# Folding the Nyquist bin of a DFT convolution into the empty sine column, and issuing one weight load later

## The chip, the cores and the metric

The kernel runs on one core of a Trainium2 chip. The metric is device time in microseconds (us) of one execution. The 13 executions of the kernel before lie within 0.3% of their median of 502.65 us (501.42 to 503.08). Every ratio below is the mean time of one kernel's fast runs over the mean of the other kernel's fast runs of the same rounds, so it is not quite the ratio of the medians that are quoted. In a profile, PE is TensorE's matmul unit, PEld its weight load, DVE is VectorE, ACT is ScalarE, and a name with q (SPq, ACTq) is that engine's queue issuing a DMA. The granted clock is the share of TensorE's full clock that the chip allowed (1.00 is full, 0.50 half). L567 is line 567 of the kernel; the changed kernel has other line numbers, so groups are best recognised by their tiles.

## The reference, cut to what matters

```python
def _A_ref(q, k, v, shift_k, ssm_k, ssm_D):       # B=1, S=2048, D=640, bf16 inputs
    k_shift = sum(k_pad[:, t:t+S, :] * shift_k[:, ks-1-t] for t in range(ks))   # 4 taps
    kv = k_shift * v
    y = irfft(rfft(pad(kv)) * rfft(pad(ssm_k)))[:S]          # causal convolution of length 2S
    return q * (y + kv * ssm_D)

x = A_q
h = x + _A_ref(layernorm(x), A_k, A_v, A_shift_k, A_ssm_k, A_ssm_D)
return h + (silu(n @ w_gate) * (n @ w_up)) @ w_down          # n = layernorm(h), F = 1728
```

## The kernel before

The convolution is done with matmuls. Even and odd time positions are two sequences of H = 1024; each is transformed with a 1024 x 1024 cosine table and a sine table, in eight blocks of 128 frequencies. The cosine half and the sine half of a block are called its two planes. The order of the work is: transposes of `ssm_k`; six "K blocks" (transform of the filter); "X blocks" (transform of kv), with the last two K blocks between them; a spectral product for each block on VectorE; the inverse transform in 16 groups, each followed by an output step on VectorE; then gate/up and down matmuls, twice.

The sine table has only 1024 frequencies, 0 to 1023. The 1025th, the Nyquist frequency, alternates +1, -1, and is done apart:

```python
def nyq_groups(src_fn, dep_all, scale, dstrow):
    for par in range(2):
        for c, (ch0, cw) in enumerate(chunks):          # chunks of 384 and 256 columns
            for tt in range(NT):                        # 8 tiles; altvec is one column of +1, -1
                tok = pe.op(... t.matmul(o, altvec, r, start=st, stop=sp_) ...)      # 32 matmuls
            atok = act.op(... a.activation(out=dst, in_=src, func=ACTF.Copy, scale=scale) ...)
...
nyqK_toks = nyq_groups(kt_chunk, t_kt_all, 0.5 / H, nyqK)     # before the first K block
...
for Fb in range(NF - NKDEF): emit_kfwd(Fb)                    # six K blocks
nyqX_toks = nyq_groups(kv_chunk, t_kv_all, 1.0, nyqX)         # before the first X block
# four one-row products on VectorE make AHrow from nyqX and nyqK
...
for Fb in range(NF):
    X_done[Fb] = fwd_block(Fb, kv_chunk, ...)                 # X block
    if Fb < NKDEF: emit_kfwd(NF - NKDEF + Fb)                 # K blocks 6 and 7
    ab_done[Fb] = spectral_products(Fb, ...)                  # VectorE
```

In the inverse, each group ends with two matmuls of one row (`altrow`, AHrow) that add the Nyquist part. The weights are loaded when the spectral products are done, all on ScalarE's queue and on one semaphore. The output step of each group uses ScalarE for a tiny square root:

```python
dma(Wg_sb, ..., s_w, deps=wdeps, eng=act)
dma(Wu_sb, ..., s_w, deps=wdeps, eng=act)
dma(Wd_sb[:, 0:NFB - 1, :], ..., s_w, deps=wdeps, eng=act)
t_wall = dma(Wd_sb[0:FL, NFB - 1, :], ..., s_w, deps=wdeps, eng=act)
...
def y_output(...):                                            # one per inverse group
    ...                                                       # L753: PSUM + kv*D, two pieces
    t_ag = dve.op(... bn_aggr ...)                            # statistics of h
    t_sq = act.op(... a.activation(out=sq2, in_=ls2[:, 1:2], func=ACTF.Sqrt, ...), deps=[t_ag, ...])
    t_rs = dve.op(... v.reciprocal ...)                       # L764, waits for the square root
    t_hn = dve.op(...)                                        # the normalised h
```

## Time and profile before

The median was 502.4 us in the first 4 runs and 502.65 us over 13.

| stage | us from the span's start | what sets the pace |
|---|---|---|
| loads, transposes, shift matmuls | 0 to 35.0 | DMA |
| K Nyquist rows | 35.0 to 41.5 | TensorE |
| six K blocks | 41.5 to 93.8 | TensorE |
| X Nyquist rows | 93.8 to 98.8 | TensorE |
| X blocks 0 to 2, K blocks 6 and 7 | 98.8 to 145 | TensorE |
| products 2 to 7 | 145.2 to 212.5 | VectorE |
| inverse and outputs | 212.6 to 309 | VectorE, 5.37 us a step |
| gate/up, down, twice | 309 to 501 | TensorE |

The page of the kernel before, part 4: the chain that ended last, followed back from the last instruction, by engine and by line, as shares of the span.

```profile
PE 61%; DVE 27%; SPq 4%; issue 2%; ACT 2%; DMA 2%; DVEq 0%
PE ps L567 19%; PE ps L877 13%; PE ps L836 12%; DVE r_x L628 11%; PE ps L834 11%; SPq L313 4%; PE ps L723 3%; DVE r_x L753 3%; DMA r_x<-in_A_k_dram 2%; PE ps L533 2%; DVE r_stage L628 2%; DVE r_x L756 2%; DVE kvt L757 2%; DVE st L759 1%; DVE r_k L765 1%
```

The removed groups (L533) are on that chain. The timeline of the kernel before around them: start, duration, engine, line, operation, tiles and shapes, count, and in brackets the idle time before the first of them and who ended it.

```profile
33.27 1.78 PE L461 MATMUL ps<-r_x,shiftm 128*128 128x384 bf16 x6 [7.57 <-DMA r_x<-in_A_k_dram]
...
34.98 5.96 PE L533 MATMUL ps<-r_k,alt 128*1 128x384 bf16 x32
...
41.49 20.70 PE L567 MATMUL ps<-r_k,tabs 128*128 128x384 bf16 x151 [0.55 <-ACT rows L536]
...
93.75 4.51 PE L533 MATMUL ps<-kvt,alt 128*1 128x384 bf16 x32
...
98.81 8.85 PE L567 MATMUL ps<-kvt,tabs 128*128 128x384 bf16 x64 [0.55 <-ACT rows L536]
```

The same 32 matmuls took 5.96 us the first time and 4.51 us the second. The reason is TensorE's clock. The view of stretches, kernel before: stretch, its length, busy time (and number of instructions) of PE, PEld, DVE, ACT and POOL, then the granted PE clock, the DMA share and GB/s.

```profile
33.00:35.00 2.00, 1.73 (x7) 0.76 (x8) 2.00 (x6) 1.20 (x4) 0.00 (x0) 0.50 1.05 395
35.00:37.00 2.00, 2.00 (x8) 0.82 (x8) 2.00 (x6) 0.89 (x3) 0.00 (x0) 0.50 1.05 386
...
39.00:41.00 2.00, 1.94 (x15) 1.02 (x13) 2.00 (x6) 0.68 (x3) 0.00 (x0) 1.00 1.05 393
```

The clock was 0.50 until some way into the stretch after 37 us.

The timeline of the kernel before, first operation of products 0, 1 and 2:

```profile
110.44 0.83 DVE L628 TENSOR_TENSOR r_x<-r_x 128x1280 bf16<-128x1280 bf16 x1 [9.19 <-ACT r_x L580]
...
127.82 0.83 DVE L628 TENSOR_TENSOR r_x<-r_x 128x1280 bf16<-128x1280 bf16 x1 [6.28 <-ACT r_x L580]
...
145.21 0.83 DVE L628 TENSOR_TENSOR r_x<-r_x 128x1280 bf16<-128x1280 bf16 x1 [6.28 <-ACT r_x L580]
```

After that the products follow one another, 11.24 us each. And the timeline of the kernel before at the start of the inverse: the issue of the W_down load, the PSUM addition (L753) of the first, second and third output, and the first square root with the reciprocal behind it.

```profile
213.61 13.22 ACTq L313 DMA_DIRECT2D r_x<-in_B_w_down_dram  x2
...
218.91 0.89 DVE L753 TENSOR_TENSOR r_x<-ps,r_x 128x384 bf16<-128x384 f32 x2 [2.88 <-PE ps L730]
...
226.87 0.29 ACT L763 ACTIVATE sqv<-lnstat,epsv 128x1 f32<-128x1 f32 x1 [30.67 <-issue]
227.20 0.16 DVE L764 RECIPROCAL lnstat<-sqv 128x1 f32<-128x1 f32 x1 [5.12 <-ACT sqv L763]
...
228.91 0.89 DVE L753 TENSOR_TENSOR r_x<-ps,r_x 128x384 bf16<-128x384 f32 x2
...
234.28 0.89 DVE L753 TENSOR_TENSOR r_x<-ps,r_x 128x384 bf16<-128x384 f32 x2
```

The W_down issue holds ScalarE's queue for 13.22 us. It is two transfers: the first, 2080 KB, was issued in 0.55 us, and the second, 80 KB and the fourth on this queue, held it from 214.19 to 226.82 (the two starts and lengths stand in the packed trace; the view merges them). The square root stands behind it in program order and runs at 226.87, although its statistics were done at 222.1. VectorE waits 5.12 us for it. From then on a step takes 5.37 us (228.91 to 234.28).

### The profile page before, as it was taken

The page shows a single profiled execution, that of the slowest core. Times are in us where ns is not written, and L with a number is a line of the kernel's source. Part 1 is how long each engine was busy: PE and PEld are TensorE (multiplying, and loading weights), DVE is VectorE, ACT ScalarE, POOL GpSimd, SP SyncE. Part 2 cuts the span into 40 slices and gives each one's busy share as a digit, 9 for nine tenths or more (in the row PEclk, how much of TensorE's full clock was granted, in tenths as well). Part 3 has the DMA queues.
Part 4 walks back from the last instruction along what each step waited for, and adds up shares of the span by engine and source line. Part 5 has one row for each costly group of instructions (what it writes and reads, how often), then busy time and mean ns, then how long its engine had stood idle before and what let it go on. Part 6 is the DMA issues. An engine that isn't in the chain of part 4 may idle for free.

```text
span 501.0 us, 6952 instructions
## 1 busy us (share of the span) xinstructions
PE 437.2 (87%) x2794; PEld 266.6 (53%) x2806; DVE 325.8 (65%) x622; ACT 134.4 (27%) x298; POOL 0.3 (0%) x5
## 2 busy tenths in 40 slices
PE   0739999999999892099999996999989999998997
PEld 0516777677777561066666662444446644443564
DVE  1499998127749999937888888666632256666122
ACT  0632444554477444000000002222200022222000
POOL 0000000000000000000000000000000000000000
PEclk9969999999999897589999999999999999999899
DMA  6999410000000000096001100000001100000011
GB/s 239 393 391 335 147 54 2 0 1 1 0 1 2 0 1 0 1 371 226 27 27 40 27 27 1 1 0 1 0 15 41 39 14 0 2 0 0 26 42 39
DMA packets 16992, 31.78 MB, mean 63 GB/s; under 512 B 1664, under 2 KB 8768, under 8 KB 16960
## 3 DMA queue, kind: packets, MB, share of 16 engines
q1 hardware_dynamic: 13888, 24.70, 14.0%
q10 hardware_dynamic: 3072, 6.64, 3.5%
q8 instruction: 22, 0.36, 0.3%
q14 instruction: 10, 0.08, 0.1%
HBM read 28.71 MB, written 2.62 MB: 63 GB/s over the span
## 4 chain that ended last, share of the span: by engine, by line
PE 61%; DVE 27%; SPq 4%; issue 2%; ACT 2%; DMA 2%; DVEq 0%
PE ps L567 19%; PE ps L877 13%; PE ps L836 12%; DVE r_x L628 11%; PE ps L834 11%; SPq L313 4%; PE ps L723 3%; DVE r_x L753 3%; DMA r_x<-in_A_k_dram 2%; PE ps L533 2%; DVE r_stage L628 2%; DVE r_x L756 2%; DVE kvt L757 2%; DVE st L759 1%; DVE r_k L765 1%
## 5 line engine op out<-in xcount | busy, mean ns | idle before, releaser
L836 PE MATMUL ps<-r_k,r_kpl 128*128 128x512 bf16 (+1 forms) x280 | 107.2, 383 | 1.0 <-DVE r_x L753 0.3
L834 PE MATMUL ps<-r_k,r_kpl 128*128 128x512 bf16 (+1 forms) x268 | 102.7, 383 | 4.2 <-DVE tabs L847 2.9
L723 PE MATMUL ps<-r_stage,tabs 128*128 128x384 bf16 (+1 forms) x512 | 73.5, 303 | 23.9 <-DVE r_stage L628 21.6
L567 PE MATMUL ps<-kvt,tabs 128*128 128x384 bf16 (+1 forms) x512 | 72.0, 304 | 3.6 <-ACT r_x L580 3.1
L723 PEld LDWEIGHTS ps<-r_stage,tabs 128*128 128x128 bf16 x512 | 49.4, 99 | 45.8 <-DVE r_stage L628 21.9
L567 PE MATMUL ps<-r_k,tabs 128*128 128x384 bf16 (+1 forms) x512 | 70.0, 300 | 0.6 <-ACT rows L536 0.6
L877 PE MATMUL ps<-r_x,tabs 128*128 128x384 bf16 x448 | 66.0, 305 | 4.0 <-DVE tabs L847 4.0
L844 DVE TENSOR_TENSOR r_kpl<-ps,r_kpl 128x512 bf16<-128x512 f32 (+1 forms) x56 | 38.7, 691 | 42.5 <-ACT r_kpl L842 42.5
L842 ACT ACTIVATE r_kpl<-ps 128x512 bf16<-128x512 f32 (+1 forms) x56 | 33.2, 597 | 120.3 <-PE ps L834 118.5
L567 PEld LDWEIGHTS ps<-kvt,tabs 128*128 128x128 bf16 x512 | 50.5, 99 | 24.8 <-ACT r_x L580 3.7
L567 PEld LDWEIGHTS ps<-r_k,tabs 128*128 128x128 bf16 x512 | 50.0, 98 | 20.2 <-issue 0.8
L877 PEld LDWEIGHTS ps<-r_x,tabs 128*128 128x128 bf16 x448 | 41.9, 99 | 28.4 <-issue 8.9
L885 DVE TENSOR_TENSOR r_x<-ps,kvt 128x384 bf16<-128x384 f32 (+1 forms) x32 | 14.2, 486 | 53.9 <-PE ps L877 53.9
L834 PEld LDWEIGHTS ps<-r_k,r_kpl 128*128 128x128 bf16 (+1 forms) x280 | 27.8, 99 | 39.0 <-DVE tabs L847 4.2
L628 DVE TENSOR_TENSOR r_x<-r_x,r_kpl 128x2560 bf16<-128x2560 bf16 x32 | 46.2, 1486 | 0.3
L628 DVE TENSOR_TENSOR r_x<-r_x 128x1280 bf16<-128x1280 bf16 x40 | 31.5, 819 | 22.4 <-ACT r_x L580 21.7
L836 PEld LDWEIGHTS ps<-r_k,r_kpl 128*128 128x128 bf16 (+1 forms) x280 | 27.8, 99 | 32.5 <-issue 1.1
L847 DVE TENSOR_TENSOR tabs<-ps,r_kpl 128x512 bf16<-128x512 f32 (+1 forms) x56 | 38.7, 691 | 1.9
L577 ACT ACTIVATE r_kpl<-ps,sck 128x384 bf16<-128x384 f32 x64 | 28.5, 528 | 40.2 <-PE ps L567 40.2
L577 ACT ACTIVATE r_x<-ps 128x384 bf16<-128x384 f32 x64 | 25.4, 458 | 33.7 <-PE ps L567 31.2
L763 ACT ACTIVATE sqv<-lnstat,epsv 128x1 f32<-128x1 f32 x16 | 4.7, 295 | 106.7 <-DVE lnstat L761 76.0
L580 ACT ACTIVATE r_x<-ps,tw 128x384 bf16<-128x384 f32 (+1 forms) x64 | 31.5, 572 | 0.0
(56 smaller groups left out, 248.5 us busy)
## 6 DMA issues: line engine op xcount, KB each, us to landing
r_stage<-in_A_k_dram SPq DMA_DIRECT2D x15, 320.0 KB, 7.4
r_k<-in_A_ssm_k_dram SPq DMA_DIRECT2D x5, 512.0 KB, 8.3
r_stage<-in_A_q_dram SPq DMA_DIRECT2D x8, 320.0 KB, 6.0
r_stage<-in_A_v_dram SPq DMA_DIRECT2D x8, 320.0 KB, 6.5
r_x<-in_A_q_dram SPq DMA_DIRECT2D x16, 160.0 KB, 2.3
out_dram<-r_x SPq DMA_DIRECT2D x16, 160.0 KB, 1.8
r_kpl<-in_B_w_gate_dram ACTq DMA_DIRECT2D x1, 2160.0 KB, 9.9
r_kpl<-in_B_w_up_dram ACTq DMA_DIRECT2D x1, 2160.0 KB, 15.2
```

What stands on the lines that cost most here:

```text
L313: return e.op_inc(lambda g, d=dst, s=src: g.dma_start(d, s), sem, 16, deps=deps)
L567: t.matmul(o, l, r, start=st, stop=sp_),
L577: atok = act.op(lambda a, o=dst, s=src, sc=sc: a.activation(out=o, in_=s, func=ACTF.Copy, scale=sc), deps=[last[gi]] + list(extra_act_deps))
L580: atok = act.op(lambda a, o=sdst[:, ch0:ch0 + cw], s=src, sc=ssc: a.activation(out=o, in_=s, func=ACTF.Copy, scale=sc), deps=list(sdeps))
L628: tt = lambda o, a, b2, op, dd: dve.op(lambda v: v.tensor_tensor(out=o, in0=a, in1=b2, op=op), deps=dd)
L723: last = pe.op(lambda t, o=o, l=lhsT, r=r, st=first: t.matmul(o, l, r, start=st, stop=False), deps=deps if (first and c == 0) else ())
L834: lastG = pe.op(lambda t, o=oG, l=lg, r=rhs, st=st, sp_=sp_: t.matmul(o, l, r, start=st, stop=sp_), deps=deps if dti == 0 else ())
L836: lastU = pe.op(lambda t, o=oU, l=lu, r=rhs, st=st, sp_=sp_: t.matmul(o, l, r, start=st, stop=sp_))
L842: t_sg = act.op(lambda a, o=sgb, s=oG: a.activation(out=o, in_=s, func=ACTF.Sigmoid), deps=[lastG, gu_pair_done.get(pidx - 3)])
L844: t_gs = dve.op(lambda v, o=gsb, s=oG, g=sgb: v.tensor_tensor(out=o, in0=s, in1=g, op=ALU.mult), deps=[t_sg, gu_pair_done.get(pidx - 3)])
L847: t_gu = dve.op(lambda v, o=dstgu, s=oU, g=gsb: v.tensor_tensor(out=o, in0=s, in1=g, op=ALU.mult), deps=[t_gs, lastU] + guT_war_deps)
L877: last = pe.op(lambda t, o=o, l=lhsT, r=r, st=first, sp_=(ft == NFB - 1): t.matmul(o, l, r, start=st, stop=sp_), deps=deps if (first and c ...
```

## The change

The sine of frequency 0 is zero at all times, so its column of the sine table carries nothing. The change puts the alternating signs there: a copy of the first 128 columns of the sine table, with that column replaced (`s0f`, 256 KB), serves block 0's sine plane, and a copy of the first 128 rows (`si0`, 256 KB) serves the inverse. The Nyquist bin then rides along in the row of frequency 0. Row 0 of the product mixes two real bins as if they were one complex bin, so it is computed again with one-row operations. The change also gives the transposes eight PSUM banks instead of four, and moves the W_down load behind the seventh inverse group, onto a semaphore of its own.

```diff
+        s0f_np = stab_f[:, 0:P].copy();  s0f_np[:, 0] = altn       # forward: block 0's sine plane
+        si0_np = stab_f[0:P, :].copy();  si0_np[0, :] = altn       # inverse: block 0's sine rows
+        def load_s0f_stab():
+            bulk_tok["s0f"] = dma(s0f[:], ..., s_s0f)               # ahead of the 2 MB sine table
+            return dma(stab, ..., s_tab2)
-                bank = tg % 4
+                bank = tg % 8
-        nyqK_toks = nyq_groups(kt_chunk, t_kt_all, 0.5 / H, nyqK)
-        nyqX_toks = nyq_groups(kv_chunk, t_kv_all, 1.0, nyqX)
-        q1 ... q4                                                    # one-row Nyquist products
+                    lhsT = s0f[:, tt, :] if (Fb == 0 and pl == 1) else tab[:, tt, Fb * P:(Fb + 1) * P]
+                  lambda Fb_, pl: (sck[:, 0:1] if Fb_ == 0 else sck[:, 1:2])   # row 0's scale 0.5/H now in both planes of K block 0
+            if Fb == 0:                                              # 8 one-row copies on ScalarE
+                scaled.setdefault((par, pl), []).append((xrow0[0:1, poff:poff + D], 1.0, []))
 ...
+            if Fb == 0:                                              # 6 one-row repairs on VectorE
+                f1 = ... xrow0 * krow0 ;  f2, f3 = ... ;  f4 = ... ;  f5, f6 = ...
 ...
-        if NFB > 1:
-            dma(Wd_sb[:, 0:NFB - 1, :], ..., s_w, deps=wdeps, eng=act)
-        t_wall = dma(Wd_sb[0:FL, NFB - 1, :], ..., s_w, deps=wdeps, eng=act)
 ...
-            for c, (ch0, cw) in enumerate(chunks):                   # inverse: two one-row matmuls a group
-                toks.append(pe.op(... t.matmul(o, altrow, r, start=False, stop=True)))
 ...
+                if qi == 6:
+                    dma(Wd_sb[:, 0:NFB - 1, :], ..., s_wd, deps=wdeps, eng=act)
+                    t_wall = dma(Wd_sb[0:FL, NFB - 1, :], ..., s_wd, deps=wdeps, eng=act)
```

More of the change, by code (lines that the diff above doesn't have):

```diff
@@ L149, in bass_sequential_preLN__ssm_conv_h3__swiglu_ffn__prompt_kernel @@
     ctab_np = _to_bf16(np.cos(ang))
-    stab_np = _to_bf16(np.sin(ang))
+    stab_f = np.sin(ang)
+    stab_np = _to_bf16(stab_f)
+    altn = (-1.0) ** np.arange(H)
+    s0f_np = stab_f[:, 0:P].copy()
+    s0f_np[:, 0] = altn
+    si0_np = stab_f[0:P, :].copy()
+    si0_np[0, :] = altn
+    s0f_np = _to_bf16(s0f_np)
+    si0_np = _to_bf16(si0_np)
     maxshift = 2
@@ L163, in bass_sequential_preLN__ssm_conv_h3__swiglu_ffn__prompt_kernel @@
     sck_np[0, 0] = 0.5 / H
-    alt_np = np.ones((P, 2 * P), dtype=np.float32)
-    alt_np[:, 0] = (-1.0) ** np.arange(P)
-    alt_np[0, P:2 * P] = (-1.0) ** np.arange(P)
-    alt_np = _to_bf16(alt_np)
     ctab_dram = nc.inline_tensor(ctab_np, name="cst_ctab")
@@ L173, in bass_sequential_preLN__ssm_conv_h3__swiglu_ffn__prompt_kernel @@
     sck_dram = nc.inline_tensor(sck_np, name="cst_sck")
-    alt_dram = nc.inline_tensor(alt_np, name="cst_alt")
+    s0f_dram = nc.inline_tensor(s0f_np, name="cst_s0f")
+    si0_dram = nc.inline_tensor(si0_np, name="cst_si0")
     bf, f32 = dt.bfloat16, dt.float32
@@ L189, in bass_sequential_preLN__ssm_conv_h3__swiglu_ffn__prompt_kernel @@
         ident = shiftm[:, 0:P]
-        alt = sb("alt", [P, 2 * P], bf)
-        altvec = alt[:, 0:1]
-        altrow = alt[0:1, P:2 * P]
         tw = sb("tw", [P, NF, 4], f32)
+        s0f = sb("s0f", [P, NT, P], bf)
+        si0 = sb("si0", [P, H], bf)
         sck = sb("sck", [P, 2], f32)
@@ L201, in bass_sequential_preLN__ssm_conv_h3__swiglu_ffn__prompt_kernel @@
         sqv2 = sb("sqv2", [P, 2, NT], f32)
-        rows = sb("rows", [P, 6 * D], bf)
-        nyqK = rows[0:1, 0:2 * D]
-        nyqX = rows[0:1, 2 * D:4 * D]
-        AHrow = rows[0:1, 4 * D:6 * D]
         NSTG = 3
@@ L220, in bass_sequential_preLN__ssm_conv_h3__swiglu_ffn__prompt_kernel @@
         a1tmp = [r_stage[:, a1tmp_off + i * D:a1tmp_off + (i + 1) * D] for i in range(4)]
-        nyqT = r_stage[0:1, a1tmp_off:a1tmp_off + 4 * D]
         AB = r_stage[:, 0:NF * 4 * D].rearrange("p (f x) -> p f x", f=NF)
@@ L231, in bass_sequential_preLN__ssm_conv_h3__swiglu_ffn__prompt_kernel @@
         NXR, NHN = 2, 3
-        sz_k = NCB * S + NHN * D
+        sz_k = NCB * S + max(NHN, 4) * D
         r_k = sb("r_k", [P, sz_k], bf)
+        xrow0 = r_k[0:1, NCB * S:NCB * S + 4 * D]
         kc = r_k[:, 0:NCB * S].rearrange("p (c s) -> p c s", c=NCB)
@@ L307, in bass_sequential_preLN__ssm_conv_h3__swiglu_ffn__prompt_kernel @@
         s_w = mksem("s_w")
+        s_wd = mksem("s_wd")
         s_xr = [mksem(f"s_xr{i}") for i in range(NXR)]
@@ L336, in kc_load @@
             kc_tok[cb] = dma(kc[:, cb, :], A_ssm_k[cb * P:(cb + 1) * P, :], s_kcb[cb])
+        s_s0f = mksem("s_s0f")
+        s_si0 = mksem("s_si0")
+        def load_s0f_stab():
+            bulk_tok["s0f"] = dma(s0f[:], s0f_dram.ap().rearrange("(t p) f -> p t f", p=P), s_s0f)
+            return dma(stab, stab_dram.ap().rearrange("(t p) f -> p t f", p=P), s_tab2)
         bulk = [
             ("ctab", lambda: dma(ctab, ctab_dram.ap().rearrange("(t p) f -> p t f", p=P), s_tab)),
-            ("stab", lambda: dma(stab, stab_dram.ap().rearrange("(t p) f -> p t f", p=P), s_tab2)),
+            ("stab", load_s0f_stab),
+            ("si0", lambda: dma(si0[:], si0_dram.ap(), s_si0)),
         ]
@@ L343, in bass_sequential_preLN__ssm_conv_h3__swiglu_ffn__prompt_kernel @@
         dma(shiftm[:], shift_dram.ap(), s_const)
-        dma(alt[:], alt_dram.ap(), s_const)
         dma(tw[:], tw_dram.ap(), s_const)
@@ L348, in bass_sequential_preLN__ssm_conv_h3__swiglu_ffn__prompt_kernel @@
         t_const = dma(Wtab[:], A_shift_k.partition_broadcast(P), s_const)
-        t_ident = t_alt = t_tw = t_sck = t_D = t_W = t_const
+        t_ident = t_tw = t_sck = t_D = t_W = t_const
         pairs = list(range(1, NT)) + [0]
@@ L520, in bass_sequential_preLN__ssm_conv_h3__swiglu_ffn__prompt_kernel @@
         t_stab = bulk_tok["stab"]
+        t_s0f = bulk_tok["s0f"]
         t_kv_all = dve.sem.cur()
-        def nyq_groups(src_fn, dep_all, scale, dstrow):
-            atoks = []
-            for par in range(2):
-                for c, (ch0, cw) in enumerate(chunks):
-                    bank = par * NCH + c
-                    deps = [dep_all, t_alt, bank_rd.get(bank)]
-                    tok = None
-                    for tt in range(NT):
-                        o = bank32(bank, 0, cw)[0:1]
-                        tok = pe.op(lambda t, o=o, r=src_fn(par, tt, c), st=(tt == 0), sp_=(tt == NT - 1):
-                                    t.matmul(o, altvec, r, start=st, stop=sp_), deps=deps if tt == 0 else ())
-                    dst = dstrow[0:1, par * D + ch0:par * D + ch0 + cw]
-                    src = bank32(bank, 0, cw)[0:1]
-                    atok = act.op(lambda a, o=dst, s=src: a.activation(out=o, in_=s, func=ACTF.Copy, scale=scale), deps=[tok])
-                    bank_rd[bank] = atok
-                    atoks.append(atok)
-            return atoks
         def kt_chunk(par, tt, c):
@@ L554, in fwd_block @@
                 base = (g2 % 2) * 4
-                deps = [dep_all, (t_ctab if pl == 0 else t_stab)]
+                deps = [dep_all, t_s0f if (Fb == 0 and pl == 1) else (t_ctab if pl == 0 else t_stab)]
                 for k4 in range(2 * NCH):
@@ L559, in fwd_block @@
                 for tt in range(NT):
-                    lhsT = tab[:, tt, Fb * P:(Fb + 1) * P]
+                    lhsT = s0f[:, tt, :] if (Fb == 0 and pl == 1) else tab[:, tt, Fb * P:(Fb + 1) * P]
                     for par in range(2):
@@ L579, in fwd_block @@
                         for (sdst, ssc, sdeps) in extra_copies:
-                            atok = act.op(lambda a, o=sdst[:, ch0:ch0 + cw], s=src, sc=ssc: a.activation(out=o, in_=s, func=ACTF.Copy, scale=sc),
+                            npart = sdst.shape[0]
+                            atok = act.op(lambda a, o=sdst[:, ch0:ch0 + cw], s=src[0:npart], sc=ssc: a.activation(out=o, in_=s, func=ACTF.Copy, scale=sc),
                                           deps=list(sdeps))
@@ L591, in emit_kfwd @@
             K_done[Fb] = fwd_block(Fb, kt_chunk, t_kt_all,
-                                   Kpl[:, Fb, :], lambda Fb_, pl: (sck[:, 0:1] if (Fb_ == 0 and pl == 0) else sck[:, 1:2]),
+                                   Kpl[:, Fb, :], lambda Fb_, pl: (sck[:, 0:1] if Fb_ == 0 else sck[:, 1:2]),
                                    extra_act_deps=[t_sck])
@@ L598, in bass_sequential_preLN__ssm_conv_h3__swiglu_ffn__prompt_kernel @@
         emit_ln1_rstd()
-        nyqX_toks = nyq_groups(kv_chunk, t_kv_all, 1.0, nyqX)
-        ndeps = nyqK_toks + nyqX_toks
-        ndeps = ndeps + [t_kv_all]
-        nxv = nyqX.rearrange("p (a x) -> p a x", a=2)
-        q1 = dve.op(lambda v: v.tensor_tensor(out=nyqT[0:1, 0:2 * D].rearrange("p (a x) -> p a x", a=2), in0=nxv,
-                                             in1=nyqK.rearrange("p (a x) -> p a x", a=2), op=ALU.mult), deps=ndeps)
-        q2 = dve.op(lambda v: v.tensor_tensor(out=nyqT[0:1, 2 * D:4 * D].rearrange("p (a x) -> p a x", a=2), in0=nxv,
-                                             in1=_rev_segments(nyqK, 2), op=ALU.mult), deps=ndeps)
-        q3 = dve.op(lambda v: v.tensor_tensor(out=AHrow[0:1, 0:D], in0=nyqT[0:1, 0:D], in1=nyqT[0:1, D:2 * D], op=ALU.subtract), deps=[q1])
-        q4 = dve.op(lambda v: v.tensor_tensor(out=AHrow[0:1, D:2 * D], in0=nyqT[0:1, 2 * D:3 * D], in1=nyqT[0:1, 3 * D:4 * D], op=ALU.add), deps=[q2])
-        t_nyq_done = q4 if q4.val > q3.val else q3
         ab_done = {}
@@ L673, in bass_sequential_preLN__ssm_conv_h3__swiglu_ffn__prompt_kernel @@
             }
+            if Fb == 0:
+                for (par, pl) in ((0, 0), (0, 1), (1, 0), (1, 1)):
+                    poff = (2 * par + pl) * D
+                    scaled.setdefault((par, pl), []).append((xrow0[0:1, poff:poff + D], 1.0, []))
             X_done[Fb] = fwd_block(Fb, kv_chunk, t_kv_all,
@@ L677, in bass_sequential_preLN__ssm_conv_h3__swiglu_ffn__prompt_kernel @@
                 emit_kfwd(NF - NKDEF + Fb)
-            ab_done[Fb] = spectral_products(Fb, Xpl[slot], Kpl[:, Fb, :], deps=[X_done[Fb], K_done[Fb], t_tw, t_nyq_done], ostok=X_done[Fb])
+            ab_done[Fb] = spectral_products(Fb, Xpl[slot], Kpl[:, Fb, :], deps=[X_done[Fb], K_done[Fb], t_tw], ostok=X_done[Fb])
+            if Fb == 0:
+                krow0 = Kpl[0:1, 0, :]
+                ab0 = AB[0:1, 0, :]
+                fx_deps = [ab_done[0], X_done[0], K_done[0]]
+                fixTb = SV1[0:1, 0:4 * D]
+                f1 = dve.op(lambda v: v.tensor_tensor(out=fixTb, in0=xrow0[0:1, 0:4 * D], in1=krow0[0:1, 0:4 * D], op=ALU.mult), deps=fx_deps)
+                f2 = dve.op(lambda v: v.tensor_tensor(out=ab0[0:1, 0:D], in0=fixTb[0:1, 0:D], in1=fixTb[0:1, 2 * D:3 * D], op=ALU.add), deps=[f1])
+                f3 = dve.op(lambda v: v.tensor_tensor(out=ab0[0:1, 2 * D:3 * D], in0=fixTb[0:1, D:2 * D], in1=fixTb[0:1, 3 * D:4 * D], op=ALU.subtract), deps=[f1])
+                f4 = dve.op(lambda v: v.tensor_tensor(out=fixTb, in0=xrow0[0:1, 0:4 * D], in1=_rev_segments(krow0[0:1, 0:4 * D], 2), op=ALU.mult), deps=[f2, f3])
+                f5 = dve.op(lambda v: v.tensor_tensor(out=ab0[0:1, D:2 * D], in0=fixTb[0:1, 0:D], in1=fixTb[0:1, 2 * D:3 * D], op=ALU.add), deps=[f4])
+                f6 = dve.op(lambda v: v.tensor_tensor(out=ab0[0:1, 3 * D:4 * D], in0=fixTb[0:1, D:2 * D], in1=fixTb[0:1, 3 * D:4 * D], op=ALU.add), deps=[f4])
+                ab_prev_reads[0] = ab_prev_reads[0] + [f5, f6]
+                t_fix = f6
         t_ab_all = ab_done[NF - 1]
@@ L682, in bass_sequential_preLN__ssm_conv_h3__swiglu_ffn__prompt_kernel @@
         dma(Wg_sb, B_w_gate.rearrange("(t p) f -> p t f", p=P), s_w, deps=wdeps, eng=act)
-        dma(Wu_sb, B_w_up.rearrange("(t p) f -> p t f", p=P), s_w, deps=wdeps, eng=act)
-        if NFB > 1:
-            dma(Wd_sb[:, 0:NFB - 1, :], B_w_down[0:(NFB - 1) * P, :].rearrange("(t p) d -> p t d", p=P), s_w, deps=wdeps, eng=act)
-        t_wall = dma(Wd_sb[0:FL, NFB - 1, :], B_w_down[(NFB - 1) * P:(NFB - 1) * P + FL, :], s_w, deps=wdeps, eng=act)
-        t_wg = t_wu = t_wd = t_wd2 = t_wall
-        inv_deps_all = [t_ab_all, t_nyq_done]
+        t_wgu = dma(Wu_sb, B_w_up.rearrange("(t p) f -> p t f", p=P), s_w, deps=wdeps, eng=act)
+        t_wg = t_wu = t_wgu
+        inv_deps_all = [t_ab_all, bulk_tok["si0"]]
         xr_free = [None] * NXR
@@ L712, in inverse_group @@
                 deps.append(bank_rd.get(bnk))
-            last = None
             first = True
             ab_c = par * D
+            nmm = NF * 2 * NCH
+            cnt = 0
+            lasts = [None] * NCH
             for Ft in range(NF):
@@ L718, in inverse_group @@
                     tab = ctab if pl == 0 else stab
-                    lhsT = tab[:, Ft, tb * P:(tb + 1) * P]
+                    lhsT = si0[:, tb * P:(tb + 1) * P] if (Ft == 0 and pl == 1) else tab[:, Ft, tb * P:(tb + 1) * P]
                     for c, (ch0, cw) in enumerate(chunks):
@@ L722, in inverse_group @@
                         r = AB[:, Ft, pl * 2 * D + ab_c + ch0:pl * 2 * D + ab_c + ch0 + cw]
-                        last = pe.op(lambda t, o=o, l=lhsT, r=r, st=first: t.matmul(o, l, r, start=st, stop=False),
-                                     deps=deps if (first and c == 0) else ())
+                        cnt += 1
+                        lasts[c] = pe.op(lambda t, o=o, l=lhsT, r=r, st=first, sp_=(cnt > nmm - NCH): t.matmul(o, l, r, start=st, stop=sp_),
+                                         deps=deps if (first and c == 0) else ())
                     first = False
-            toks = []
-            for c, (ch0, cw) in enumerate(chunks):
-                o = bank32(banks[c], 0, cw)
-                r = AHrow[0:1, par * D + ch0:par * D + ch0 + cw]
-                toks.append(pe.op(lambda t, o=o, r=r: t.matmul(o, altrow, r, start=False, stop=True)))
-            return banks, toks[-1]
+            return banks, lasts[-1]
         def y_output(qi, par, tb, banks, ytok):
@@ L806, in bass_sequential_preLN__ssm_conv_h3__swiglu_ffn__prompt_kernel @@
                     x_reload(qi + NXR)
+                if qi == 6:
+                    if NFB > 1:
+                        dma(Wd_sb[:, 0:NFB - 1, :], B_w_down[0:(NFB - 1) * P, :].rearrange("(t p) d -> p t d", p=P), s_wd, deps=wdeps, eng=act)
+                    t_wall = dma(Wd_sb[0:FL, NFB - 1, :], B_w_down[(NFB - 1) * P:(NFB - 1) * P + FL, :], s_wd, deps=wdeps, eng=act)
+                    t_wd = t_wd2 = t_wall
                 gi += 1
```

## The prediction

> **What bounds the kernel now.** The chain of waits shows four stages in series. (1) TensorE from 33.3 us, when the last small input lands: shift matmuls, K Nyquist rows (32 one-column matmuls, 35.0 to 41.0), six K blocks (41.5 to 93.8), X Nyquist rows (93.8 to 98.3), then X and deferred K blocks to 142.7. (2) VectorE: six spectral products back to back, 145.2 to 212.5. (3) Inverse transform to 304: VectorE's output steps, one per 5.37 us (timeline); TensorE needs 4.5 us for a group's 32 matmuls, 0.44 for the Nyquist pair, 0.45 for transposes, just less. (4) Gate/up and down matmuls, TensorE-bound, to 501.
>
> **What the change does.**
> - Removes the K Nyquist matmuls (5.9 us plus a 0.55 us wait for ScalarE) and the X ones (4.45 plus 0.55). All lie on the chain, but not all is won. The windows show the granted clock at 0.5 from 33 to 37.5 us, and the removed matmuls sat in 2.5 us of that. [...] So the K blocks inherit the slow stretch: about 1.4 us given back. Win 5.0 + 5.0 = 10.0 us. VectorE's kv phase ends at 85.2, before X starts at about 88.8.
> - Removes 32 Nyquist matmuls from the inverse groups (10 us busy). Hidden behind VectorE's 5.37 us step, except in the first group: 0.4 us.
> - Moves the W_down load behind the seventh group, off the weights' semaphore. Its issue holds ScalarE's queue from 213.6 to 226.8 (timeline), so the first tiny square root runs at 226.9 and VectorE waits 5.1 us for it, once (waits). VectorE sets the pace afterwards, so this is never recovered. Without it the second output's addition moves from 228.9 to about 223.5; TensorE, now slightly behind, takes back about 0.5. Win 4.9 us.
> - Adds, in X block 0, eight one-row copies on ScalarE (0.37 us each by the present row copies: 1.5 per plane). ScalarE then needs 4.6 us per plane against TensorE's 4.35: a stall of about 0.4.
> - Adds six one-row VectorE operations after product 0. A row costs what 128 do (1x1280 took 0.815 us, 128x1280 0.819), so 4.8 us, but VectorE idles 6.3 us before product 1 and again before product 2. Cost: zero.
> - Adds two 256 KB loads. The first is needed by K block 0's second plane at about 40.7; the loads ahead of it land at 37.0, so I estimate 38.5. The larger table lands a microsecond after 43.2, needed at 49.
> - Eight transpose banks instead of four: the shift matmuls still wait for a load until 33.2. Zero.
>
> **Sum.** 502.4 - 10.0 - 0.4 - 4.9 + 0.4 - 0.2 (one small load fewer) = **487.3 us**; 8 in 10: 484.5 to 490.8. Chances: faster by over 2% 0.93, within 2% 0.06, slower 0.01.
>
> **What would show it.** First K matmul near 35 us, at clock 0.5 for 2 to 3 us; first X matmul near 88.8; still 6 x 11.24 us of products before the inverse, which starts near 203; first square root within 1 us of its statistics; output steps still 5.37 us, VectorE-paced; gate/up and down unchanged. Wrong would be: K block 0 waiting for the small sine table, steps below 5.3 us, or products 1 or 2 waiting on the row repairs.
>
> **What would make it wrong.** The small table's 256-byte rows landing after 41 us, the W_down issue blocking ScalarE again, or the slow clock returning elsewhere.

A mark shows where a sentence was cut; no term of the sum is cut with it, and it comes to 487.3 us as it stands. That the K blocks inherit the slow stretch, and the 1.4 us given back for it, was the author's estimate from the 2.5 us of clock 0.50 in which, by the view of stretches, the removed matmuls sat (35.0 to 37.5; the clock record has the half clock until 37.97). The prediction gives no source for the 0.2 us of the small load.

## More of the kernel before

The trace's clock record has half clock from 27.73 us, while TensorE idled (25.70 to 33.27), until 37.97. From the first shift matmul at 33.27 until then TensorE was busy without a break, for 4.70 us. What brings the full clock back is not shown by this.

## The result, and the profile after

The changed kernel took 486.02 us, median of 8 runs (485.7 to 488.29), against 502.65 us before. The ratio of the fast runs is 0.9685, 95% interval 0.967 to 0.9699: 3.1% faster. The output passes the correctness test, which does not see a missing frequency (below), so it does not show that the Nyquist bin is right. The page of the changed kernel, part 4:

```profile
PE 59%; DVE 29%; SPq 4%; issue 3%; ACT 2%; DMA 2%; DVEq 0%
PE ps L557 20%; PE ps L873 14%; PE ps L832 12%; DVE r_x L607 12%; PE ps L830 11%; SPq L314 4%; DVE r_x L744 3%; DMA r_x<-in_A_k_dram 2%; DVE r_x L747 2%; DVE kvt L748 2%; DVE st L750 2%; DVE r_stage L607 2%; DVE r_k L756 1%; DVE r_x L738 1%
```

The L533 share of the chain is gone. The timeline of the changed kernel: first plane of K block 0, its second plane (which reads `s0f`), and the first X matmuls.

```profile
34.77 6.23 PE L557 MATMUL ps<-r_k,tabs 128*128 128x384 bf16 x32 [0.33 <-ACT r_x L473]
...
40.84 4.51 PE L557 MATMUL ps<-r_k,s0f 128*128 128x384 bf16 x32
...
88.66 4.51 PE L557 MATMUL ps<-kvt,tabs 128*128 128x384 bf16 x32
```

X starts 10.15 us earlier (98.81 to 88.66). K block 0's first plane took 6.23 us and its second 4.51, for the same number of matmuls. The view of stretches of the changed kernel shows that the half clock moved onto it:

```profile
35.00:37.00 2.00, 2.00 (x9) 1.21 (x8) 2.00 (x7) 0.29 (x2) 0.00 (x0) 0.50 1.13 378
37.00:39.00 2.00, 2.00 (x12) 1.21 (x11) 2.00 (x7) 0.00 (x0) 0.00 (x0) 0.67 1.06 410
39.00:41.00 2.00, 2.00 (x16) 1.41 (x15) 2.00 (x6) 0.34 (x1) 0.00 (x0) 1.00 1.04 390
```

The timeline of the changed kernel between products 0 and 1: the first and the last row repair, and the first operation of product 1.

```profile
112.62 1.48 DVE L667 TENSOR_TENSOR r_x<-r_k,r_kpl 1x2560 bf16<-1x2560 bf16 x1
...
117.05 0.47 DVE L672 TENSOR_TENSOR r_stage<-r_x 1x640 bf16<-1x640 bf16 x1
117.68 0.83 DVE L607 TENSOR_TENSOR r_x<-r_x 128x1280 bf16<-128x1280 bf16 x1 [0.16 <-ACT r_x L571]
```

The repairs fill the gap almost exactly: product 1 still waits for ScalarE, by 0.16 us. Product 2 starts at 135.06, 46.40 us after the first X matmul, as before (145.21 - 98.81 = 46.40). At the inverse (timeline of the changed kernel; the last line is the W_down issue in its new place):

```profile
208.51 0.89 DVE L744 TENSOR_TENSOR r_x<-ps,r_x 128x384 bf16<-128x384 f32 x2 [2.69 <-PE ps L719]
...
211.72 0.30 ACT L754 ACTIVATE sqv<-lnstat,epsv 128x1 f32<-128x1 f32 x1 [25.67 <-DVE lnstat L752]
...
213.75 0.89 DVE L744 TENSOR_TENSOR r_x<-ps,r_x 128x384 bf16<-128x384 f32 x2
...
219.12 0.89 DVE L744 TENSOR_TENSOR r_x<-ps,r_x 128x384 bf16<-128x384 f32 x2
...
243.82 1.37 ACTq L314 DMA_DIRECT2D r_x<-in_B_w_down_dram  x2
```

The first square root runs 3.2 us after the addition that it belongs to, not 8.0, and the W_down issue takes 1.37 us where no other weight load stands in front of it. The step is still 5.37 us (213.75 to 219.12), so the one-row matmuls that left the inverse bought nothing there.

| milestone, us | before | after | difference |
|---|---|---|---|
| first X matmul | 98.81 | 88.66 | -10.15 |
| first inverse matmul | 212.58 | 202.43 | -10.15 |
| first output's addition | 218.91 | 208.51 | -10.40 |
| second output's addition | 228.91 | 213.75 | -15.16 |
| 16th output's addition | 304.10 | 288.94 | -15.16 |
| first gate product on VectorE | 309.54 | 294.38 | -15.16 |
| first down matmul | 369.21 | 352.49 | -16.72 |
| span | 501.0 | 484.3 | -16.7 |

The table shows a step that the prediction did not foresee: between the first gate product and the first down matmul another 1.56 us are saved, where the change touches nothing. In both kernels TensorE waits there once for VectorE, for 2.88 us. The view of stretches, kernel before, around the end of that wait:

```profile
308.00:311.00 3.00, 0.13 (x1) 0.00 (x0) 1.70 (x4) 2.47 (x4) 0.00 (x0) 1.00 0.00 0
311.00:313.00 2.00, 1.99 (x5) 0.73 (x6) 1.97 (x4) 0.00 (x0) 0.00 (x0) 0.51 0.03 8
```

and the changed kernel at the same place:

```profile
293.00:296.00 3.00, 0.14 (x1) 0.11 (x2) 1.70 (x4) 2.32 (x4) 0.00 (x0) 1.00 0.00 0
296.00:298.00 2.00, 2.00 (x10) 0.88 (x9) 1.97 (x4) 0.00 (x0) 0.00 (x0) 1.00 0.00 0
```

The clock fell to 0.51 behind this wait in the one profile and stayed at 1.00 in the other. What differed is read from the two traces under "Where half-clock stretches fell".

### The profile page after: what moved, and what is told of

It reads as the page before. It is cut to its first block, busy times and chain, and to the rows that moved or that the text cites. A ratio compares the mean times of both kernels' runs of the same rounds, so it can differ in the third digit from the quotient of the medians.

```text
span 484.3 us, 6766 instructions
## 1 busy us (share of the span) xinstructions
PE 416.6 (86%) x2698; PEld 259.8 (54%) x2710; DVE 328.1 (68%) x624; ACT 133.7 (28%) x298; POOL 0.3 (0%) x5
## 4 chain that ended last, share of the span: by engine, by line
PE 59%; DVE 29%; SPq 4%; issue 3%; ACT 2%; DMA 2%; DVEq 0%
PE ps L557 20%; PE ps L873 14%; PE ps L832 12%; DVE r_x L607 12%; PE ps L830 11%; SPq L314 4%; DVE r_x L744 3%; DMA r_x<-in_A_k_dram 2%; DVE r_x L747 2%; DVE kvt L748 2%; DVE st L750 2%; DVE r_stage L607 2%; DVE r_k L756 1%; DVE r_x L738 1%; DVE st L751 1%
## 5 line engine op out<-in xcount | busy, mean ns | idle before, releaser
L719 PE MATMUL ps<-r_stage,tabs 128*128 128x384 bf16 x480 | 71.4, 303 | 26.6 <-DVE r_stage L607 21.6
L719 PEld LDWEIGHTS ps<-r_stage,tabs 128*128 128x128 bf16 x480 | 46.6, 99 | 46.2 <-DVE r_stage L607 21.9
L557 PE MATMUL ps<-kvt,tabs 128*128 128x384 bf16 x480 | 67.7, 304 | 3.1 <-ACT r_x L571 3.1
L557 PE MATMUL ps<-r_k,tabs 128*128 128x384 bf16 x480 | 67.6, 304 | 0.3 <-ACT r_x L473 0.3
L840 DVE TENSOR_TENSOR r_kpl<-ps,r_kpl 128x512 bf16<-128x512 f32 (+1 forms) x56 | 38.7, 691 | 40.8 <-ACT r_kpl L838 40.8
L557 PEld LDWEIGHTS ps<-kvt,tabs 128*128 128x128 bf16 x480 | 47.4, 99 | 22.9 <-ACT r_x L571 3.7
L557 PEld LDWEIGHTS ps<-r_k,tabs 128*128 128x128 bf16 x480 | 47.6, 99 | 20.1 <-issue 1.2
```

The source lines that it names most:

```text
L557: t.matmul(o, l, r, start=st, stop=sp_),
L719: lasts[c] = pe.op(lambda t, o=o, l=lhsT, r=r, st=first, sp_=(cnt > nmm - NCH): t.matmul(o, l, r, start=st, stop=sp_), deps=deps if (first ...
L840: t_gs = dve.op(lambda v, o=gsb, s=oG, g=sgb: v.tensor_tensor(out=o, in0=s, in1=g, op=ALU.mult), deps=[t_sg, gu_pair_done.get(pidx - 3)])
```

## The experiments

Twelve kernels ran, each for five rounds against the kernel before on the same chip, and each gave one profile. All passed the correctness test (a missing frequency at this size does not show in it).

### e1: only the W_down move, in the kernel before

```diff
-        dma(Wd_sb...) x2, on s_w, after the products
+                if qi == 6: dma(Wd_sb...) x2, on s_wd
```

> The kernel before, with only the W_down load moved behind the seventh inverse group and onto its own semaphore. Theory (the load's issue blocks ScalarE's queue, VectorE loses 5.1 us once at the first square root and never regains it): about 4.7 us less, 497.9 us; the first square root runs within 1 us of its statistics; the steps stay at 5.37 us. Rival (TensorE sets the pace of the inverse, the wait of VectorE is slack): within 0.5 us of before, 502.4.

Measured: 498.33 us against 502.57, ratio 0.9917 (0.9903 to 0.993). The move alone made the kernel 4.2 us faster. The second output's addition comes 12.81 us after the first inverse matmul (224.54 - 211.73), not 16.33 as before, although the first group ran longer at half clock here (its addition came after 7.57 us, not 6.33). The third step was longer; the timeline of e1, second addition, the copy out of the transposes, third addition:

```profile
224.54 0.89 DVE L751 TENSOR_TENSOR r_x<-ps,r_x 128x384 bf16<-128x384 f32 x2
...
229.34 0.49 DVE L781 COPY r_k<-ps 128x640 bf16<-128x640 bf16 x1 [0.61 <-PE ps L777]
...
230.62 0.89 DVE L751 TENSOR_TENSOR r_x<-ps,r_x 128x384 bf16<-128x384 f32 x2
```

That step took 6.08 us, because VectorE waited 0.61 us for a transpose that TensorE did behind its third group with its Nyquist pair. So where VectorE is no longer held up, the one-row matmuls do cost about 0.6 us, once. In the changed kernel, without them, this wait does not occur. The third addition came 18.89 us after the first inverse matmul, against 21.70 before: 2.8 us are seen there, and the rest lies in half-clock stretches that fell elsewhere.

### e2: the changed kernel with W_down back in its old place

```diff
+        dma(Wd_sb...) x2, on s_w, after the products
-                if qi == 6: dma(Wd_sb...) x2, on s_wd
```

> The changed kernel with the W_down load back in its old place. Theory: the 5.1 us wait for the first square root is back, 4.8 us lost, about 490.9 us. Rival (the load's place is worth nothing, the gain is all Nyquist work): 486.

Measured: 490.74 us, against 486.02 for the changed kernel in its own rounds (ratios to before 0.9763 and 0.9685). The loss is 4.7 us by the medians and 3.9 by the ratios (0.0078 of 502.5), near the expected 4.8, but not for the expected reason alone. The issue held ScalarE's queue for 12.11 us in this profile, and VectorE waited for the square root again, though 3.17 us and not 5.1, because the first group, at half clock, ended later (7.17 us after the first inverse matmul, 6.08 in the changed kernel):

```profile
214.69 0.16 DVE L758 RECIPROCAL lnstat<-sqv 128x1 f32<-128x1 f32 x1 [3.17 <-ACT sqv L757]
```

The second addition came 15.22 us after the first inverse matmul, against 11.32 in the changed kernel, 3.9 us later. Besides, X started 1.27 us earlier and gate/up took 1.58 us longer, by the half clock. So the move was seen from both sides: about 4 us won when it is made alone, 4 to 5 lost when it alone is undone. The sign and the wait are shown; the size changes with what the clock does beside it.

### e3: the kernel before without the inverse's one-row matmuls (wrong result)

```diff
-            toks.append(pe.op(... t.matmul(o, altrow, r, start=False, stop=True)))     # 32 matmuls
```

> The kernel before without the 32 one-row Nyquist matmuls of the inverse groups (a wrong result on purpose: one frequency is missing). Theory (hidden behind VectorE's step of 5.37 us): at most 0.4 us less, 502.1 us, steps still 5.37 us. Rival (TensorE's 10 us of them are on the path): 7 to 10 us less, 493 to 495 us.

Measured: 502.12 against 502.57 us, ratio 0.9995 (0.9977 to 1.0013). The rival falls: these 32 matmuls are 9.6 us of busy TensorE time in the groups of the kernel before, and nothing came of their removal, because VectorE's step of 5.37 us stood beside it. The first group, where 0.4 us were expected, cannot be judged here, as the second output still waits for ScalarE's queue.

### e4: the kernel before without the two forward groups (wrong result)

```diff
-        nyqK_toks = nyq_groups(...)      -        nyqX_toks = nyq_groups(...)
+        t_nyq_done = pool.op(lambda g: g.memset(AHrow, 0.0))
```

> The kernel before without both forward groups of one-column Nyquist matmuls; the inverse reads a row of zeros in their place (a wrong result on purpose). Theory: first K matmul at about 34.9 us, X at about 88.8, and about 10.1 us less, 492.3 us; not the 12.3 us that the removed groups and their waits span, because the first K block then runs the half clock that they ran. Rival (VectorE's products hide it): under 3 us.

Measured: 494.6 against 502.57 us, 8.0 us less, not 10.1. The mechanism holds, but the expectation missed a new wait. PE in the timeline of e4: the first plane of K block 0, then its second plane with the blocks behind it:

```profile
35.22 5.44 PE L567 MATMUL ps<-r_k,tabs 128*128 128x384 bf16 x32 [0.33 <-ACT r_x L465]
43.34 14.89 PE L567 MATMUL ps<-r_k,tabs 128*128 128x384 bf16 x96 [2.68 <-DMA tabs<-cst_stab]
```

With the first K block 6 us earlier, its second plane comes before the 2 MB sine table has landed, and TensorE waits 2.68 us; the 96 matmuls behind that wait took 14.89 us, where 124 of them take 17.01 us in the changed kernel (45.19 to 62.20), which is 13.2 for 96: 1.7 us were lost there besides, about what the half-clock stretch in gate/up costs (1.56). X started at 92.84, not at about 88.8. In the changed kernel that plane reads the small block `s0f`, which was queued ahead of the large table and landed at 37.1 us. So `s0f` is not only a place for the Nyquist column: it also lets the earlier start be used.

### e5: the changed kernel without row copies and row repairs (wrong result)

```diff
-                scaled.setdefault((par, pl), []).append((xrow0[0:1, poff:poff + D], 1.0, []))
-                f1 ... f6
```

> The changed kernel without the eight one-row copies on ScalarE and the six one-row repairs on VectorE (a wrong result on purpose: row 0 of the product mixes two frequencies). Theory (4.9 us of VectorE work that lies in its idle time between products 0 and 1): no change, 486.0 us within 0.5; product 2 starts at the same distance from the first X matmul, 46.4 us, and product 1 waits about 5 to 6 us for ScalarE again. Rival (the repairs are on the path): 4 to 5 us less, 481.5.

Measured: 486.13 us, ratio 0.9689, against 0.9685 for the changed kernel. The 4.9 us of VectorE work (112.62 to 117.52) cost nothing, as they lie in its idle time: without them product 1 waited 6.28 us for ScalarE, and product 2 started 46.41 us after the first X matmul, as expected.

### e6: the changed kernel with the small sine block behind the large table

```diff
-            s0f load, then stab load
+            stab load, then s0f load
```

> The changed kernel with the 256 KB sine block queued behind the 2 MB sine table instead of ahead of it. Theory (K block 0 started early enough only because this block lands at 37 us; the run without the forward rows waited 2.7 us there for the large table): K block 0's second plane waits about 3 us, until about 43.5 us, and all after it is 2 to 3.5 us later: 488 to 489.5 us. Rival (the missing 2 us of that run were clock luck): 486.0 within 0.5.

Measured: 492.49 us, ratio 0.9802: 6.4 us lost, more than the 2 to 3.5 expected. PE in the timeline of e6 shows the wait and what it did:

```profile
34.81 5.86 PE L558 MATMUL ps<-r_k,tabs 128*128 128x384 bf16 x32 [0.33 <-ACT r_x L474]
43.62 6.19 PE L558 MATMUL ps<-r_k,s0f 128*128 128x384 bf16 x32 [2.95 <-DMA s0f<-cst_s0f]
```

The wait was 2.95 us, as expected, and the plane behind it took 6.19 us instead of 4.51: the clock fell to half again. X started at 93.12, 4.5 us later than in the changed kernel. The other 2 us of the profile lie at the first inverse group (0.8 us longer) and after the first gate product (1.3 us longer), where half-clock stretches fell. The sign and the wait confirm e4's reading. Of the loss, 4.5 us are the wait and the half clock directly behind it; the other 2 us come from where later half-clock stretches fell.

### e7 and e9: unread matmuls ahead of the K blocks

```diff
-                bank = tg % 8                          # transposes
+                bank = tg % 6                          # frees a bank for the unread matmuls
+        for _ in range(30):        # e9: 52
+            pe.op(lambda t: t.matmul(bank32(7, 0, 384), ident, shiftm[:, 0:384], start=True, stop=True), ...)
         emit_shift_matmuls()
```

> The changed kernel with 30 matmuls that nobody reads, into a free PSUM bank, while TensorE waits for the last small input. Theory (K block 0 runs its first microseconds at the half clock that the Nyquist rows ran before): K block 0's first plane takes 4.3 instead of 5.9 us, X starts at about 87.0, about 1.5 us less, 484.5 us. If the clock falls back in the gap after the extra matmuls, nothing is won. Rival (the slow first plane waits for data, not the clock): 486.0 within 0.5.

> As e7, with 52 extra matmuls instead of 30, so that at the 168 ns each that e7 showed they last until about 32.5 us, just before the shift matmuls at 33.2. Theory (e7 won nothing because TensorE stood idle for 4.4 us after its extra matmuls and the clock fell to half again): full clock throughout, K block 0's first plane takes 4.3 to 4.5 us instead of 5.9, X starts at about 87.1, 1.5 us earlier than in the changed kernel; in the time of the whole kernel 484.5 us, give or take a later half-clock window of 1.6 us. Rival (the slow first plane is not the clock): first plane 5.9 us still.

Measured, e7: 487.7 us, ratio 0.9714 (0.9687 to 0.9741), 1.7 us slower than the changed kernel. Its extra matmuls ran at full clock, 30 in 5.04 us, and ended at 28.8; TensorE then idled 4.4 us, the stretch from 34 to 38 us ran at clock 0.50, and the first plane took 6.58 us. Measured, e9: 487.12 us, again no gain in the median, with single runs at 484.0 and 485.5 (both at mean clock 0.972, the highest of the five fast ones) and 487.1 to 488.4 (0.965 to 0.968). Its profile (span 496.6 us at mean clock 0.923) is not compared with fast ones. So whether the first plane can be rid of the half clock was not settled by these two; e12 settled it.

### e8 and e10: the second deferred K block later

```diff
-            if Fb < NKDEF: emit_kfwd(NF - NKDEF + Fb)
+            if Fb in (0, 2): emit_kfwd(NF - NKDEF + Fb // 2)        # e10: (0, 3), Fb // 3
```

> The changed kernel with the second deferred K block after X block 2 instead of after X block 1. Theory (VectorE's products set the pace and idle 6.3 us before product 2 only because that K block stands ahead of X block 2): products 1 to 7 follow one another without a gap, the inverse starts about 6 us earlier, 480.0 us. Here the row repairs would be on the path. Rival (TensorE sets the pace of this stage): 486.

> As e8, with the second deferred K block one block later still, after X block 3. Theory (e8 won only 2.6 of the 6.3 us because its K block stood ahead of X block 3, for which VectorE then idled 3.7 us): the products follow without any gap, the inverse starts at about 196.3 us, 6.1 us earlier than in the changed kernel. The time is then 480 us plus up to 3 us, because TensorE idles before the inverse and after the first gate/up matmuls[...]: 480 to 483. Rival (VectorE's stage cannot be shortened so): 486.

Measured, e8: 485.89 us, a miss. First operations of products 2 and 3 in the timeline of e8:

```profile
128.86 0.83 DVE L607 TENSOR_TENSOR r_x<-r_x 128x1280 bf16<-128x1280 bf16 x1
...
143.70 0.82 DVE L607 TENSOR_TENSOR r_x<-r_x 128x1280 bf16<-128x1280 bf16 x1 [3.73 <-ACT r_x L571]
```

Product 2 no longer waits, but product 3 does, 3.73 us, because the K block now stands ahead of X block 3. The inverse started at 199.83, 2.6 us earlier, and half-clock stretches took the rest: the first inverse group needed 7.32 us to the first addition instead of 6.08, and gate/up was 1.5 us longer. Measured, e10: 480.32 us (480.04 to 480.98), ratio 0.9563. The inverse started at 196.74, 5.7 us earlier than in the changed kernel, near the expected 196.3.

### e11 and e12: combined

e11 is e10 with K block 0 ahead of the shift matmuls (and `s0f` loaded before the cosine table), and with unread matmuls at two waits of TensorE: 23 behind an early operation of product 7, 12 ahead of the fourth gate/up pair. e12 adds 34 between the transposes and K block 0, and puts the transposes on six banks as e7 does.

```diff
+        emit_kfwd(0)                                   # e12: 34 unread matmuls ahead of this line
         emit_shift_matmuls()
-            ("ctab", ...), ("stab", s0f and stab), ("si0", ...)
+            ("s0f", ...), ("ctab", ...), ("stab", stab alone), ("si0", ...)
+        for i in range(23): unread matmul, deps=[third operation of product 7]     # ahead of the inverse
+                    if par == 0 and pidx == 3:         # gate/up
+                        for _ in range(12): unread matmul
```

> A try at a better version: the changed kernel with e10's order, with the small sine block loaded before the cosine table and K block 0 ahead of the shift matmuls (so that K starts when its table lands, near 29 us, and X when VectorE's kv phase ends, near 84.8), with 23 unread matmuls on TensorE during the last 7.5 us of product 7 and 12 in the wait of 2.9 us in gate/up, to keep the clock up. Theory: 4 us from the start, 6.1 from the order of K7, 1.5 from the warm first inverse group, up to 1.6 from gate/up: 473 to 476 us. If the extra matmuls don't hold the clock, 476 to 479.

> e11 with 34 further unread matmuls between the transposes and K block 0. In e11 the first plane of K block 0 took 6.9 us at the half clock, after TensorE had idled 6.2 us, and X started at 86.7, while VectorE's kv phase ended at 84.4. Theory (the extra matmuls follow the transposes at full clock, as e7 and e9 showed, and end at about 28.3, just before the cosine table lands at 28.7): first plane 4.4 us, X at about 84.5, 2 us less than e11: 475.5 us, give or take one half-clock window of 1.6 us. Rival (the clock falls anyway, as in e9): 477.5.

Measured, e11: 477.56 us, ratio 0.9514. The expected 473 to 476 were missed. The extra matmuls ahead of the inverse worked: the first addition came 4.56 us after the first inverse matmul, against 6.61 in e10. The earlier K start gave only 1.4 us at X (86.67 against 88.05), because K block 0's first plane took 7.24 us (the expectation of e12 says 6.9), 5.6 of them at half clock, after a wait of 6.15 us for the table. Measured, e12: 475.49 us (473.76 to 475.77), ratio 0.9445 (0.9425 to 0.9466); it is the fastest of all. PE in the timeline of e12: the extra matmuls, the two planes of K block 0, the next K block.

```profile
24.12 5.69 PE L584 MATMUL ps<-shiftm 128*128 128x384 bf16 x34
29.77 4.51 PE L554 MATMUL ps<-r_k,tabs 128*128 128x384 bf16 x32
34.11 4.51 PE L554 MATMUL ps<-r_k,s0f 128*128 128x384 bf16 x32
...
41.52 14.77 PE L554 MATMUL ps<-r_k,tabs 128*128 128x384 bf16 x95 [1.95 <-ACT r_x L474]
```

K block 0's first plane now takes 4.51 us, so the slow first plane was the clock. But X still starts at 86.65: K block 1 waits 1.95 us until ScalarE has emptied the shift matmuls' banks, and the clock fell to 0.54 between 42 and 44 us. The expected 84.5 was missed. The gain over e11 came later: from the first to the second down stage e12 took 94.80 us and e11 96.47, and from there to the end 35.3 and 37.0, because e11 has a half-clock stretch at each of them and e12 has none. So the time met the expectation, but not for the expected reason: nothing that e12 adds aims at the down stages, and this gain over e11 is luck as far as shown.

### Where half-clock stretches fell

The trace's clock record gives each grant with its length. In the profiles of before and after, the half-clock stretches while the kernels work lasted 3.41, 10.24, 13.65 and 20.48 us, which is 1, 3, 4 and 6 times 3.413. TensorE has three waits behind the inverse: 2.9 us in the first gate/up, before the fourth pair, and about 2.0 us before each down stage. Where the clock record has a half-clock stretch just behind them, by profile (fast only):

```
                      gate/up   first down   second down
before                  yes         -           yes
after                    -          -           yes
e1, e3, e7, e10          -         yes           -
e2, e4, e6, e8          yes         -           yes
e5                       -          -           yes
e11 (gate/up filled)     -         yes          yes
e12 (gate/up filled)     -          -            -
```

The wait in gate/up is 2.9 us in all of the first eleven profiles, and five of them fell to half clock behind it. Those five need 59.3 to 59.7 us from the first gate product to the first down matmul, the other six 58.0 to 58.2. Of the 26 waits of about 2.0 us before a down stage, 13 had a half-clock stretch behind them. Executions of one kernel differ too: those of the changed kernel spread from a span of 483.9 us at mean clock 0.961 to 486.5 at 0.954. All four fast runs of e10 had 0.964 and the five of e12 0.978 to 0.986, but the six of e3 lie between 0.956 and 0.966.

What differed between the profiles of before and after can be read from their two clock records. In each, all changes of the clock from 24 us to the end of the work lie whole multiples of 3.413 us apart (to 0.01 us): the first at 27.73 us in before and at 24.67 in after. Continue them as a grid of lines every 3.413 us, cut the three waits behind the inverse at these lines, and take the longest piece. In the three waits with a half-clock stretch behind them that piece is 2.88 us (gate/up, before) and 1.99 us (second down stage, in both); in the other three it is 1.54 us (gate/up, after), 1.84 and 1.96 us (first down stage, before and after). For the wait in gate/up:

| | before | after |
|---|---|---|
| TensorE idle, us from the span's start | 308.13 to 311.01 | 292.98 to 295.86 |
| lines of the grid around it | 307.62, 311.04 | 290.91, 294.32, 297.73 |
| idle between two lines | 2.88 | 1.34 and 1.54 |
| clock behind it | 0.50 from 311.04 to 314.45 | 1.00 |

So the wait lay between two lines in the one profile and was cut in two by a line in the other. This is a pattern in six waits of two profiles, found afterwards; no run moved a wait on purpose to test it, and why the clock changed on such lines is not shown. Elsewhere the length alone does not tell: a wait of 1.95 us ahead of K block 1 was followed by half clock in e12 (0.54 from 42 to 44 us) and not in e11 (124 matmuls in 17.00 us), and in the profile of after the idle time ahead of the shift matmuls has a first piece of 1.95 us (22.71 to 24.67) with half clock right behind it. Nor are the 12 unread matmuls in gate/up shown to have won anything: 58.1 us from the first gate product to the first down matmul is also what the unfilled profiles without a stretch there took.

## Why the prediction was right

The prediction was 487.3 us, the result 486.02, inside the range of 484.5 to 490.8. Point by point:

- **Forward Nyquist groups, 10.0 us predicted.** X started 10.15 us earlier, which includes the 0.2 predicted for one small load fewer. The argument that part of the 11.45 us is given back to the half clock holds. The size was a little more than the predicted 1.4: K block 0's first plane took 6.23 us against 4.51, so 1.7, because the half clock lasted until 37.97 us in before and 38.32 in after, and not 37.5. In e12, which differs from e11 here only by extra matmuls ahead (and the six transpose banks), that plane took 4.51 us, and in e11 7.24.
- **Inverse matmuls hidden but for 0.4 us.** The first addition gained 0.25 us, the step stayed at 5.37, and e3 shows no effect in the kernel before (0.9995). Right.
- **W_down, 4.9 us.** The second addition moved by 5.01 us relative to the first inverse matmul, 0.25 of it from the term above, so 4.76. e1 (4.2 us) and e2 (4.7 by the medians, 3.9 by the ratios) see it alone, with different half-clock stretches behind it. The predicted 0.5 us that TensorE would take back did not appear in the changed kernel, only in e1 (0.61 us), where the one-row matmuls remain; so the removal of those matmuls was worth that half microsecond. That the term came out so near is in part luck. The prediction was 5.4 (228.9 to 223.5) less 0.5; the second addition came 5.24 us after the first, by VectorE's own operations, and not 4.6 as 223.5 has it, so the gain was 4.76 less nothing.
- **A stall of 0.4 us by ScalarE in X block 0.** It did not occur. A plane took ScalarE 4.29 us (92.82 to 97.11), not 4.6, just below TensorE's 4.35. This term was mis-sized.
- **Row repairs, zero.** Right, with 0.16 us to spare; e5 confirms it.
- **Small sine block in time.** Predicted at 38.5, landed at 37.1, used at 40.8. e4 and e6 show that this was no detail: without it, or behind the large table, TensorE waits 2.7 to 2.95 us and loses clock besides.
- **Eight transpose banks, zero.** Not tried by itself. In both profiles the shift matmuls wait for a load until about 33 us, well after the transposes, so the banks had no visible way to show.

At the second output the terms predict 10.0 + 0.4 + 4.9 - 0.4 + 0.2 = 15.1 us, and the profiles show 15.16. What the prediction lacked is the remaining 1.56 us: one half-clock stretch in gate/up that the profile of before has and that of after has not. It named such a thing only as a risk, "the slow clock returning elsewhere". It is not an accident of the two profiles alone, as the medians differ by 16.6 us like the spans (16.7). But nothing in the change aims at it, the wait ahead of it is 2.88 us in both, and undoing the unrelated W_down move (e2) brought the stretch back while making that move alone (e1) took it away and gave another at the first down stage. What differed in the traces is that a line of the 3.413 us grid cut the wait in the profile of after and none did in that of before. Nothing on which the prediction rested tells where these lines would lie, so these 1.56 us are luck; without them the time would have been about 487.6, still next to 487.3. Why the runs of one kernel agree as far as they do is not shown.

## What to carry to other kernels

Ask of each removed instruction which engine paced the place where it stood: 64 one-column matmuls were worth 10 us, 32 one-row ones in a stage paced by VectorE at most 0.6, and the place of one DMA issue 4 to 5, because a tiny operation of the pacing engine's chain stood behind it in the same queue. When work moves earlier, look what it then waits for (here a 2 MB table, saved by a 256 KB piece loaded first). And a wait of TensorE of two or three microseconds may cost another 1.1 to 1.7 us of half clock behind it: here 13 of 26 waits of about 2.0 us and 5 of 11 of 2.9 us had such a stretch behind them. From 486.0 to 475.5 us, 5.7 came from a better order of one block, about 2 from unread matmuls ahead of the inverse and 1.4 from the earlier start; the rest is where half-clock stretches happened to fall.
